# Each half of TensorE's rows makes its own chunks of F, and no PSUM bank has two writers: a change to a routed expert kernel

## Chip, cores and metric

One core of one Trainium2 chip. The metric is the device time of one execution in microseconds (us); the kernel before takes 1424.76 us (median, 1422.38 to 1425.43).

## The reference, cut to what matters

A causal depthwise convolution over 7 positions, then a mixture of 8 experts in which each token goes to one expert.

```python
B, S, D, E, F = (8, 3584, 192, 8, 1024)     # 28,672 tokens
# for each token, with e its expert and p the softmax of its logits:
h = np.maximum(x[b, s] @ w1[e], 0.0)        # first product: 192 -> 1024
out[b, s] = p[e] * (h @ w2[e])              # second product: 1024 -> 192
# e is argmax(logits), or the previous token's expert where the local gate says so
```

Everything is float32. The convolution, the choice of experts and the sorting of tokens into the experts' slots come first for each group of tokens; then blocks of 128 or 256 tokens of one expert run through the two products.

## The kernel before

There are 144 blocks: 35 of 128 tokens, 87 of 256, 22 of 128. TensorE is used as two halves of 64 rows each (`rows = slice(half * 64, half * 64 + 64)`), which run beside each other. `turn` transposes the gathered rows, `hidden` makes the first product and the Relu, `output` the second product in two runs (`part` 0 and 1), `send` scales and scatters. `step` puts pieces of convolution and routing of later groups between the blocks' own work. `P` = 128, `DR` = 64, `FK` = 8 chunks of F, `KT` = 2; `n` is the block's tokens over 128.

```python
    def turn(n, xg):
        xps = xps_p.tile([P, 2, 512], F32, name="xps")
        at = xps.rearrange("p h (d k s) -> p h d k s", d=4, k=2)
        for d in range(2):
            for k in range(n):
                for half in range(2):
                    turn_half(at[:, half, d, k, :],
                              xg[:, k, Y0 + d * P:Y0 + (d + 1) * P], half)
        xT = tp.tile([P, 2, BT], F32, name="xT")
        to = xT.rearrange("p d (k h s) -> p h d k s", k=KT, h=2)
        if n == KT:
            nc.vector.tensor_copy(to.rearrange("p h d k s -> p h (d k) s"),
                                  xps[:, :, :BT].rearrange("p h (x s) -> p h x s", s=DR))
        else:
            nc.vector.tensor_copy(to[:, :, :, 0, :], at[:, :, :2, 0, :])
        return xT
```

192 channels are 128 + 64. To give the last 64 channels a partner on the other half, `xg` holds them twice, and each half takes other chunks of F for them. So in the first product both halves add into the same bank, at different times, and each bank is handed from one half to the other:

```python
    ORDER = [[(0, 0), (1, 0), (0, 1), (1, 1), (4, 0), (5, 0), (2, 0), (3, 0),
              (6, 0), (7, 0), (6, 1), (7, 1)],
             [(2, 0), (3, 0), (2, 1), (3, 1), (6, 0), (7, 0), (0, 0), (1, 0),
              (4, 0), (5, 0), (4, 1), (5, 1)]]
    BANKS = [0, 1, 2, 3]
    def pass_by(last_of):
        seen = nc.scalar.nop()
        for half in range(2):
            tc.add_manual_dep(seen.ins, last_of[half], SYNC, reason="the bank's")
        return seen
    def hidden(n, wb, xT):
        hT = hp.tile([P, FK, BT], F32, name="hT")
        hps = {b: hps_p.tile([P, 2, BT], F32, name="hps") for b in BANKS}
        w = slice(0, n * P)
        left = {b: 6 for b in BANKS}
        passed = {}
        last_of = {}
        for at in range(len(ORDER[0])):
            for half in range(2):
                f, last = ORDER[half][at]
                rows = slice(half * DR, (half + 1) * DR)
                f0 = F + (f % 2 + f // 4 * 2) * P if last else f * P
                b = f // 2
                mm = nc.tensor.matmul(hps[b][:, f % 2, w], lhsT=wb[rows, f0:f0 + P],
                                      rhs=xT[rows, last, w], start=(left[b] == 6),
                                      stop=(left[b] <= 2), skip_group_check=True)
                if at in passed:
                    tc.add_manual_dep(mm.ins, passed[at].ins.name, SYNC, reason="its bank")
                last_of[half] = mm.ins.name
            if at in (3, 5):
                passed[6 if at == 3 else 8] = pass_by(last_of)
            for half in range(2):
                f, last = ORDER[half][at]
                b = f // 2
                left[b] -= 1
                if not left[b]:
                    nc.scalar.activation(hT[:, 2 * b:2 * b + 2, w], hps[b][:, :, w], Act.Relu)
        return hT
    def output(n, wb, hT, yps, part, done):
        for m in range(FK):
            if n == 1 and m // 4 != part:
                continue
            for half in range(2):
                rows = slice(half * DR, (half + 1) * DR)
                k = (part + half) % 2 if n == KT else 0
                mm = nc.tensor.matmul(yps[half if n == 1 else k][:, :D],
                                      lhsT=hT[rows, m, k * P:(k + 1) * P],
                                      rhs=wb[rows, WA + m * D:WA + (m + 1) * D],
                                      start=(m == 0 and not part),
                                      stop=(m == FK - 1 and part == 1), skip_group_check=True)
                if n == KT and part and m == 0:
                    tc.add_manual_dep(mm.ins, done["passed"].ins.name, SYNC, reason="its bank")
                done[half] = mm.ins.name
        if not part and n == KT:
            done["passed"] = pass_by(done)
    def send(n, xg, yps):
        o_sb = op.tile([P, KT, D], F32, name="o_sb")
        for k in range(n):
            gate = xg[:, k, 0:1]
            nc.scalar.activation(o_sb[:, k, :], yps[k][:, :D], Act.Copy, scale=gate)
            if n == 1:
                nc.vector.scalar_tensor_tensor(o_sb[:, 0, :], yps[1][:, :D], gate, o_sb[:, 0, :],
                                               Alu.mult, Alu.add)
            nc.gpsimd.nop()
            # ... indirect DMA of o_sb[:, k, :] to the tokens' rows

```

A hand-over is a ScalarE no-operation that waits for the last matmul of both halves (`pass_by`), and a matmul that waits for it. The second product of a block of 256 has one hand-over as well: in part 0 the first half works for tokens 0 to 127 and the second for 128 to 255, in part 1 the other way round. The loop over blocks:

```python
    for i, (_, n, _, _) in enumerate(blocks):
        ensure(i)
        weights(i + AHEAD)
        hT = hidden(n, wbs[i], xT)
        yps = [yps_p.tile([P, 512], F32, name="yps") for half in range(2)]
        done = {}
        output(n, wbs[i], hT, yps, 0, done)
        if i + 1 < len(blocks):
            xT = turn(blocks[i + 1][1], xgs[i + 1])
        step(0.8 * n, 1)
        output(n, wbs.pop(i), hT, yps, 1, done)
        send(n, xgs.pop(i), yps)
        step(3.2 * n, n)
```

Note the place of `turn`: between part 0 and part 1 of the second product.

## Time and profile before

| | before |
|---|---|
| timed | 1424.76 us |
| first profile, span | 1538.3 us |
| second profile of the same kernel, span (taken later, below) | 1421.5 us |
| late block of 256 / of 128 tokens, start to start | 10.90 / 5.64 us |

The prediction was made from the first profile alone, and its lines are shown there. It was an odd execution, as the experiments found. The same kernel's second profile is the one to compare with; from here on "before" in a profile means the second. Its page opens so:

```profile
span 1421.5 us, 40261 instructions
...
PE 1388.2 (98%) x16670; PEld 1278.9 (90%) x16670; DVE 659.0 (46%) x1773; ACT 497.5 (35%) x1168; POOL 503.6 (35%) x524
```

TensorE is busy all the time but for 33 us, some 20 of them before the first block. Next are its table of waits (total us, times, longest us), first for the waits on ScalarE, and its late blocks in the timeline of TensorE (start, length, line, operation, output and inputs, sizes, count):

```profile
PEld yps L680 <- ACT hT L670: 14.5, 88, 0.4
...
PE yps L680 <- ACT hT L670: 0.2, 1, 0.2
```

```profile
1204.01 5.35 PE L657 MATMUL hps<-xT,wb 64*128 64x256 f32 x48
1209.19 2.90 PE L680 MATMUL yps<-wb,hT 64*128 64x192 f32 x32
1211.93 0.41 PE L263 MATMUL xps<-ident,xg 64*128 64x64 f32 x8
1212.21 2.87 PE L680 MATMUL yps<-wb,hT 64*128 64x192 f32 x32
1214.91 5.35 PE L657 MATMUL hps<-xT,wb 64*128 64x256 f32 x48
```

Read the timeline from start to start. Sixteen steps of the second product take 2.74 us in the first run (1209.19 to 1211.93), where 16 x 0.1625 would be 2.60. And the table of waits has 88 weight loads of the second product (PEld yps) that wait for the Relu, about 0.16 us each: one for nearly every block of 256. The other half is a like wait at the start of the second product in blocks of 128, shown with the run e_first.

### The profile page before, as it was taken

The page shows a single profiled execution, that of the slowest core. Times are in us where ns is not written, and L with a number is a line of the kernel's source. Part 1 is how long each engine was busy: PE and PEld are TensorE (multiplying, and loading weights), DVE is VectorE, ACT ScalarE, POOL GpSimd, SP SyncE. Part 2 cuts the span into 40 slices and gives each one's busy share as a digit, 9 for nine tenths or more (in the row PEclk, how much of TensorE's full clock was granted, in tenths as well). Part 3 has the DMA queues.
Part 4 walks back from the last instruction along what each step waited for, and adds up shares of the span by engine and source line. Part 5 has one row for each costly group of instructions (what it writes and reads, how often), then busy time and mean ns, then how long its engine had stood idle before and what let it go on. Part 6 is the DMA issues. An engine that isn't in the chain of part 4 may idle for free.

```text
span 1538.3 us, 40261 instructions
## 1 busy us (share of the span) xinstructions
PE 1416.7 (92%) x16670; PEld 1278.5 (83%) x16670; DVE 657.0 (43%) x1773; ACT 500.3 (33%) x1168; POOL 502.2 (33%) x524
## 2 busy tenths in 40 slices
PE   7589988999998999999999999998999999999998
PEld 4378988988887787888778887887899999999998
DVE  7557766665665555665565655122000000000111
ACT  3224343342433333343343333322222222222232
POOL 1342335343333334434344343433422121212111
PEclk9899999999999999999999999999999999999999
DMA  4488879866474665656566554555555555556893
GB/s 159 164 318 329 311 280 367 301 268 245 178 281 172 228 223 187 239 192 239 208 222 234 173 193 173 188 171 185 207 206 176 197 183 190 187 180 216 310 322 142
DMA packets 66472, 343.93 MB, mean 224 GB/s; under 512 B 12656, under 2 KB 23655, under 8 KB 45810
## 3 DMA queue, kind: packets, MB, share of 16 engines
q1 hardware_dynamic: 44064, 288.66, 53.4%
q0 software_dynamic: 22224, 52.70, 8.9%
q8 instruction: 131, 2.15, 0.6%
q14 instruction: 51, 0.42, 0.1%
q10 hardware_dynamic: 2, 0.00, 0.0%
HBM read 288.51 MB, written 53.49 MB: 222 GB/s over the span
## 4 chain that ended last, share of the span: by engine, by line
PE 58%; issue 28%; POOL 6%; ACT 4%; another core or an unknown queue 2%; DVE 1%; DMA 0%; POOLq 0%; ACTq 0%; DVEq 0%
PE hps L657 26%; PE yps L680 24%; POOL out_dram L701 4%; ACT hT L670 3%; PE hps L263 2%; PE hps L307 2%; PE xps L263 1%; POOL slots L466 1%; PE yps L184 1%; PE hps L184 1%; DMA x_sb<-in_x_dram 0%; DVE y_sb L201 0%; PE hps L406 0%; POOLq L701 0%
## 5 line engine op out<-in xcount | busy, mean ns | idle before, releaser
L680 PE MATMUL yps<-wb,hT 64*128 64x192 f32 x7392 | 683.7, 330 | 61.5 <-ACT hT L670 45.7
L680 PEld LDWEIGHTS yps<-wb,hT 64*128 64x128 f32 x7392 | 597.3, 187 | 105.4 <-ACT hT L670 72.7
L657 PE MATMUL hps<-xT,wb 64*128 64x256 f32 (+1 forms) x6912 | 648.6, 339 | 22.5 <-ACTq L639 19.6
L657 PEld LDWEIGHTS hps<-xT,wb 64*128 64x128 f32 x6912 | 565.9, 189 | 83.2 <-ACTq L639 29.8
L701 POOL DMA_INDIRECT out_dram<-o_sb,xg x231 | 232.5, 1006 | 902.6 <-ACT o_sb L695 630.1
L670 ACT ACTIVATE hT<-hps 128x512 f32<-128x512 f32 (+1 forms) x576 | 267.3, 511 | 462.4 <-PE hps L657 376.4
L201 DVE SCALAR_TENSOR_TENSOR y_sb<-x_sb,c,y_sb 128x336 f32<-128x336 f32 x720 | 403.2, 570 | 22.4 <-ACT y_sb L176 4.2
L623 DVE COPY xT<-xps 128x512 f32<-128x512 f32 x87 | 60.2, 692 | 611.6 <-PE xps L263 611.6
L466 POOL DMA_INDIRECT slots<-y_sb,posi x224 | 230.4, 1029 | 107.7 <-issue 85.2
L695 ACT ACTIVATE o_sb<-yps,xg 128x192 f32<-128x192 f32 x231 | 87.7, 418 | 360.2 <-PE yps L680 360.2
L626 DVE COPY xT<-xps 128x256 f32<-128x256 f32 x57 | 24.2, 424 | 131.9 <-PE xps L263 123.8
L300 ACT COPY yT<-hps 128x512 f32<-128x512 f32 x93 | 50.1, 592 | 60.5 <-PE hps L263 50.7
L176 ACT ACTIVATE y_sb<-x_sb,c 128x336 f32<-128x336 f32 x116 | 64.8, 580 | 15.1 <-PE yps L680 14.7
L263 PEld LDWEIGHTS xps<-ident,xg 64*128 64x128 f32 x924 | 52.6, 139 | 2.6
L263 PE MATMUL xps<-ident,xg 64*128 64x64 f32 x924 | 52.2, 221 | 0.0
L697 DVE SCALAR_TENSOR_TENSOR o_sb<-yps,xg,o_sb 128x192 f32<-128x192 f32 x57 | 23.8, 418 | 58.0 <-ACT o_sb L695 51.2
L307 PE MATMUL hps<-yT,wg 128*32 128x256 f32 (+1 forms) x384 | 25.9, 376 | 7.4 <-issue 7.4
L307 PEld LDWEIGHTS hps<-yT,wg 128*32 128x32 f32 x384 | 12.1, 111 | 16.2 <-issue 10.8
L263 PE MATMUL hps<-ident,y_sb 64*128 64x64 f32 x512 | 21.2, 223 | 2.6 <-DVE y_sb L201 1.5
L263 PEld LDWEIGHTS hps<-ident,y_sb 64*128 64x128 f32 x512 | 19.8, 139 | 4.0 <-issue 2.7
L184 PE MATMUL hps<-x_sb,wb 128*128 128x336 f32 x56 | 18.1, 489 | 3.7 <-DMA x_sb<-in_x_dram 3.7
L272 POOL COPY yr<-y_sb 128x896 f32<-128x896 f32 x15 | 14.4, 961 | 18.0 <-ACT y_sb L187 18.0
(142 smaller groups left out, 370.3 us busy)
## 6 DMA issues: line engine op xcount, KB each, us to landing
wb<-in_w_dram SPq DMA_DIRECT2D x144, 1536.0 KB
x_sb<-in_x_dram SPq DMA_DIRECT2D x16, 1920.0 KB
xg<-slots SPq DMA_DIRECT2D x87, 258.0 KB
xg<-slots SPq DMA_DIRECT2D x57, 129.0 KB
out_dram<-o_sb,xg POOLq DMA_INDIRECT x231
slots<-y_sb,posi POOLq DMA_INDIRECT x224
slots<-pad SPq DMA_DIRECT2D x1, 129.0 KB
slots<-pad,toi POOLq DMA_INDIRECT x8
```

The costliest lines, as they stand in the source:

```text
L176: nc.scalar.activation(cols(h), chans(h, 0), Act.Copy, scale=c[:, h, 0:1])
L201: nc.vector.scalar_tensor_tensor(cols(h), chans(h, k), c[:, h, k:k + 1], cols(h), Alu.mult, Alu.add)
L263: nc.tensor.transpose(to, src[rows, :], identity=ident[rows, rows])
L300: copy(to[:, :, half * DR:(half + 1) * DR], tps[half])
L307: nc.tensor.matmul(lps[32 * j:32 * j + 32, :w], lhsT=wg[:, u, :], rhs=yT[:, u, j, :w], start=(u == 0), stop=(u == 2))
L466: ins = nc.gpsimd.indirect_dma_start(out=slots[:, :], in_=rows, in_offset=None, out_offset=bass.IndirectOffsetOnAxis(ap=to, axis=0)).ins
L623: nc.vector.tensor_copy(to.rearrange("p h d k s -> p h (d k) s"), xps[:, :, :BT].rearrange("p h (x s) -> p h x s", s=DR))
L657: mm = nc.tensor.matmul(hps[b][:, f % 2, w], lhsT=wb[rows, f0:f0 + P], rhs=xT[rows, last, w], start=(left[b] == 6), stop=(left[b] <= 2), s ...
L670: nc.scalar.activation(hT[:, 2 * b:2 * b + 2, w], hps[b][:, :, w], Act.Relu)
L680: mm = nc.tensor.matmul(yps[half if n == 1 else k][:, :D], lhsT=hT[rows, m, k * P:(k + 1) * P], rhs=wb[rows, WA + m * D:WA + (m + 1) * D], ...
L695: nc.scalar.activation(o_sb[:, k, :], yps[k][:, :D], Act.Copy, scale=gate)
L701: sent = nc.gpsimd.indirect_dma_start(out=out, in_=o_sb[:, k, :], in_offset=None, out_offset=bass.IndirectOffsetOnAxis(ap=xg.bitcast(I32)[ ...
```

## The change

Its intent: no bank has two writers, so no hand-over is needed. Each half holds all 192 channels as three thirds of 64, of overlapping pairs: channels 0 to 63 and 64 to 127, 64 to 127 and 128 to 191, 128 to 191 and again 0 to 63, so that each half sees every third once. It makes its own four chunks of F in its own banks; in the second product each half sums its own rows of all chunks in its own bank, and VectorE adds the two sums. The price is three transposes for two. The transposes move to between the two products, and the stepped-in work is split 2.1 and 2.1 in place of 0.8 and 3.2.

```diff
@@ -610,92 +611,64 @@
 
     def turn(n, xg):
 
+
         xps = xps_p.tile([P, 2, 512], F32, name="xps")
-        at = xps.rearrange("p h (d k s) -> p h d k s", d=4, k=2)
-        for d in range(2):
+        at = xps[:, :, :KD * BT // 2].rearrange("p h (d k s) -> p h d k s", d=KD, k=KT)
+        for d in range(KD):
             for k in range(n):
+                src = xg[:, k, Y0 + d * DR:Y0 + (d + 2) * DR]
                 for half in range(2):
-                    turn_half(at[:, half, d, k, :],
-                              xg[:, k, Y0 + d * P:Y0 + (d + 1) * P], half)
-        xT = tp.tile([P, 2, BT], F32, name="xT")
+                    turn_half(at[:, half, d, k, :], src, half)
+        xT = tp.tile([P, KD, BT], F32, name="xT")
         to = xT.rearrange("p d (k h s) -> p h d k s", k=KT, h=2)
         if n == KT:
             nc.vector.tensor_copy(to.rearrange("p h d k s -> p h (d k) s"),
-                                  xps[:, :, :BT].rearrange("p h (x s) -> p h x s", s=DR))
+                                  at.rearrange("p h d k s -> p h (d k) s"))
         else:
-            nc.vector.tensor_copy(to[:, :, :, 0, :], at[:, :, :2, 0, :])
+            nc.vector.tensor_copy(to[:, :, :, 0, :], at[:, :, :, 0, :])
         return xT
 
-
-
-    ORDER = [[(0, 0), (1, 0), (0, 1), (1, 1), (4, 0), (5, 0), (2, 0), (3, 0),
-              (6, 0), (7, 0), (6, 1), (7, 1)],
-             [(2, 0), (3, 0), (2, 1), (3, 1), (6, 0), (7, 0), (0, 0), (1, 0),
-              (4, 0), (5, 0), (4, 1), (5, 1)]]
-    BANKS = [0, 1, 2, 3]
-
-    def pass_by(last_of):
-
-        seen = nc.scalar.nop()
-        for half in range(2):
-            tc.add_manual_dep(seen.ins, last_of[half], SYNC, reason="the bank's")
-        return seen
+    def halves():
+        return [(half, slice(half * DR, (half + 1) * DR)) for half in range(2)]
 
     def hidden(n, wb, xT):
         hT = hp.tile([P, FK, BT], F32, name="hT")
-        hps = {b: hps_p.tile([P, 2, BT], F32, name="hps") for b in BANKS}
         w = slice(0, n * P)
-        left = {b: 6 for b in BANKS}
-        passed = {}
-        last_of = {}
-        for at in range(len(ORDER[0])):
+
+
+        for two in range(2):
+            hps = [hps_p.tile([P, 2, BT], F32, name="hps") for half in range(2)]
+            for d in range(KD):
+                for j in range(2):
+                    f0 = (d * 4 + two * 2 + j) * P
+                    for half, rows in halves():
+                        nc.tensor.matmul(hps[half][:, j, w], lhsT=wb[rows, f0:f0 + P],
+                                         rhs=xT[rows, d, w], start=(d == 0 and j == 0),
+                                         stop=(d == KD - 1), skip_group_check=True)
             for half in range(2):
-                f, last = ORDER[half][at]
-                rows = slice(half * DR, (half + 1) * DR)
-                f0 = F + (f % 2 + f // 4 * 2) * P if last else f * P
-                b = f // 2
-                mm = nc.tensor.matmul(hps[b][:, f % 2, w], lhsT=wb[rows, f0:f0 + P],
-                                      rhs=xT[rows, last, w], start=(left[b] == 6),
-                                      stop=(left[b] <= 2), skip_group_check=True)
-                if at in passed:
-                    tc.add_manual_dep(mm.ins, passed[at].ins.name, SYNC, reason="its bank")
-                last_of[half] = mm.ins.name
-            if at in (3, 5):
-                passed[6 if at == 3 else 8] = pass_by(last_of)
-            for half in range(2):
-                f, last = ORDER[half][at]
-                b = f // 2
-                left[b] -= 1
-                if not left[b]:
-                    nc.scalar.activation(hT[:, 2 * b:2 * b + 2, w], hps[b][:, :, w], Act.Relu)
+                m = half * 4 + two * 2
+                nc.scalar.activation(hT[:, m:m + 2, w], hps[half][:, :, w], Act.Relu)
         return hT
 
-    def output(n, wb, hT, yps, part, done):
-        for m in range(FK):
-            if n == 1 and m // 4 != part:
-                continue
-            for half in range(2):
-                rows = slice(half * DR, (half + 1) * DR)
-                k = (part + half) % 2 if n == KT else 0
-                mm = nc.tensor.matmul(yps[half if n == 1 else k][:, :D],
-                                      lhsT=hT[rows, m, k * P:(k + 1) * P],
-                                      rhs=wb[rows, WA + m * D:WA + (m + 1) * D],
-                                      start=(m == 0 and not part),
-                                      stop=(m == FK - 1 and part == 1), skip_group_check=True)
-                if n == KT and part and m == 0:
-                    tc.add_manual_dep(mm.ins, done["passed"].ins.name, SYNC, reason="its bank")
-                done[half] = mm.ins.name
-        if not part and n == KT:
-            done["passed"] = pass_by(done)
-
-    def send(n, xg, yps):
+    def output(n, wb, xg, hT):
+
+        yps = [yps_p.tile([P, 512], F32, name="yps") for half in range(2)]
+        for m4 in ([0, 1, 4, 5], [2, 3, 6, 7]):
+            for k in range(n):
+                for m in m4:
+                    for half, rows in halves():
+                        nc.tensor.matmul(yps[half][:, k * D:(k + 1) * D],
+                                         lhsT=hT[rows, m, k * P:(k + 1) * P],
+                                         rhs=wb[rows, WA + m * D:WA + (m + 1) * D],
+                                         start=(m == 0 and k == 0), stop=(m == FK - 1),
+                                         skip_group_check=True)
         o_sb = op.tile([P, KT, D], F32, name="o_sb")
         for k in range(n):
             gate = xg[:, k, 0:1]
-            nc.scalar.activation(o_sb[:, k, :], yps[k][:, :D], Act.Copy, scale=gate)
-            if n == 1:
-                nc.vector.scalar_tensor_tensor(o_sb[:, 0, :], yps[1][:, :D], gate, o_sb[:, 0, :],
-                                               Alu.mult, Alu.add)
+            y = [yps[half][:, k * D:(k + 1) * D] for half in range(2)]
+            nc.scalar.activation(o_sb[:, k, :], y[0], Act.Copy, scale=gate)
+            nc.vector.scalar_tensor_tensor(o_sb[:, k, :], y[1], gate, o_sb[:, k, :],
+                                           Alu.mult, Alu.add)
```

```diff
@@ -816,24 +789,19 @@
         ensure(i)
         weights(i + AHEAD)
         hT = hidden(n, wbs[i], xT)
-        yps = [yps_p.tile([P, 512], F32, name="yps") for half in range(2)]
-        done = {}
-        output(n, wbs[i], hT, yps, 0, done)
         if i + 1 < len(blocks):
             xT = turn(blocks[i + 1][1], xgs[i + 1])
-        step(0.8 * n, 1)
-        output(n, wbs.pop(i), hT, yps, 1, done)
-        send(n, xgs.pop(i), yps)
-        step(3.2 * n, n)
+        step(2.1 * n, 1)
+        output(n, wbs.pop(i), xgs.pop(i), hT)
+        step(2.1 * n, n)
 
 
 def _w1_layout(np, w1):
 
 
-    rest = w1[:, P:, :].reshape(E, DR, FK, P)
-    rest = np.stack([rest[:, :, [0, 1, 6, 7]], rest[:, :, [2, 3, 4, 5]]], 1)
-    rest = rest.reshape(E, P, F // 2)
-    return np.concatenate([w1[:, :P, :], rest], 2)
+    w = w1.reshape(E, KD, DR, 2, F // 2).transpose(0, 3, 2, 1, 4)
+    w = np.stack([w[:, 0], w[:, 1][:, :, [1, 2, 0]]], 1)
+    return w.reshape(E, P, KD * F // 2)
```

(The remaining edits only set sizes and the copied 64 channels.)

More of the change, by code (lines that the diff above doesn't have):

```diff
@@ L31 @@
 NX = NT + HALO
-DR = D - P
+DR = P // 2
+KD = D // DR
 FK = F // P
@@ L54 @@
 GQ = (NP + 3) // 4
-WA = F + F // 2
+WA = F * KD // 2
 WB = FK * D
@@ L262, in turn_half @@
         rows = slice(half * DR, (half + 1) * DR)
-        nc.tensor.transpose(to, src[rows, :], identity=ident[rows, rows])
+        nc.tensor.transpose(to, src[rows], identity=ident[rows, rows])
     def route(g, alone):
@@ L273, in route @@
         if not (alone and g):
-            copy(y_sb[:, :, Y0 + D:], y_sb[:, :, Y0 + P:Y0 + D])
+            copy(y_sb[:, :, Y0 + D:], y_sb[:, :, Y0:Y0 + DR])
         def leave(*pairs):
@@ L312, in route @@
         if alone and g:
-            copy(y_sb[:, :, Y0 + D:], y_sb[:, :, Y0 + P:Y0 + D])
+            copy(y_sb[:, :, Y0 + D:], y_sb[:, :, Y0:Y0 + DR])
         yield "hop"
```

## The prediction

> **What bounds the kernel now.** I read the page first, then the table of waits, then the table of stretches, then the timeline of one late block, in that order.
>
> ```profile
> span 1538.3 us, 40261 instructions
> PE 1416.7 (92%) x16670; PEld 1278.5 (83%) x16670; DVE 657.0 (43%) x1773; ACT 500.3 (33%) x1168; POOL 502.2 (33%) x524
> ...
> DVE  7557766665665555665565655122000000000111
> ```
>
> TensorE is the bound: 92% busy, everything else under half. VectorE works only in the first two thirds, where the convolution and the routing run beside the expert blocks. The first thing to see is the span: the profiled execution took 1538 us, the timed ones 1424.76. The profile is 8% slower than what is to be predicted, so part of what it shows is not in the timed run.
>
> ```profile
> PEld yps L680 <- ACT hT L670: 72.7, 108, 2.3
> ...
> PE yps L680 <- ACT hT L670: 45.7, 57, 2.0
> ...
> PEld hps L657 <- ACTq L639: 29.8, 29, 2.1
> ...
> PE hps L657 <- ACTq L639: 19.6, 21, 1.8
> ```
>
> These are the waits that the change aims at (total, times, longest). The second product (L680) waits for the Relu; the first product (L657) waits for the ScalarE no-operation (L639) that passes a PSUM bank from one half of the rows to the other.
>
> ```profile
> 79.90:327.90 248.00, 226.55 (x3265) 212.09 (x3265) 168.20 (x441) 96.25 (x258) 96.64 (x95) 0.98 0.87 320
> 327.90:1123.00 795.10, 730.73 (x8160) 648.32 (x8159) 402.70 (x1106) 267.71 (x589) 310.59 (x306) 1.00 0.59 206
> 1123.00:1406.90 283.90, 283.90 (x3124) 265.10 (x3122) 17.71 (x26) 75.44 (x156) 51.56 (x53) 1.00 0.54 187
> ```
>
> The columns are stretch, length, busy time of PE, its weight loads, DVE, ACT and POOL, clock, DMA share, GB/s. The first is 35 blocks of 128 tokens, the next two are the 87 blocks of 256 tokens, and 22 blocks of 128 follow. In the third stretch PE is busy for all of its 283.90 us: there are no idle gaps at all. The waits lie in the first two stretches.
>
> ```profile
> 1287.00 5.35 PE L657 MATMUL hps<-xT,wb 64*128 64x256 f32 x48
> ...
> 1292.18 2.91 PE L680 MATMUL yps<-wb,hT 64*128 64x192 f32 x32
> ...
> 1294.92 0.41 PE L263 MATMUL xps<-ident,xg 64*128 64x64 f32 x8
> ...
> 1295.20 2.87 PE L680 MATMUL yps<-wb,hT 64*128 64x192 f32 x32
> ...
> 1297.90 5.35 PE L657 MATMUL hps<-xT,wb 64*128 64x256 f32 x48
> ```
>
> One late block of 256 tokens runs from 1287.00 to 1297.90: 10.90 us. The two row halves run in pairs, so 48 instructions are 24 steps. From start to start: first product 5.18 us (24 steps of 0.216), second product 2.74 (16 steps of 0.1625 are 2.60, and 0.14 over), transposes 0.28 (4 steps of 0.0615, and 0.03 over), second product 2.70 (2.60 and 0.10 over). The single records put the 0.14 at the ninth step of the second product, where it meets the last Relu, and the 0.10 at its first step after the transposes. The same reading of a late block of 128 tokens gives 5.64 us: 24 steps of 0.112, 16 of 0.1625, 2 of 0.0615, and 0.23 over.
>
> **What the Trainium skill says.** "TensorEngine Tiling (Array Packing)", Gotcha 1, PSUM pressure: different row tiles must not be in the same PSUM bank at once, and software has to see to it. That is why the kernel before has its L639 hand-overs, and why a kernel whose halves never share a bank may drop them. "Perfetto Trace Analysis", section on the per-instruction lifecycle: the end of a TensorE instruction in a profile is a model, made from its size. The trace agrees: 48 instructions that start 0.216 us apart in pairs are recorded as 0.376 us each, which is why I count from start to start. "TensorE: Matmul & The Clock Gate", back-to-back issue gap, lists 262 cycles for 256 columns, an estimate of 0.109 us at its 2.4 GHz; the trace has 0.216 for one of the two float32 instructions of a matmul, and I use the trace.
>
> **The change, part by part.**
> 1. Products: the same number and sizes. First product before 12 matmuls per half, after 3 channel thirds by 4 chunks, also 12. Second product 8 chunks per half and 128 tokens in both. Cost 0.
> 2. Transposes: three overlapping pairs of 64 channels instead of two. A block of 256 has 6 steps for 4, a block of 128 has 3 for 2. 87 x 2 x 0.0615 + 57 x 0.0615 = 10.7 + 3.5 = +14.2 us, all on TensorE's path.
> 3. Overheads in a block. The transposes move to between the two products, so the Relu of the first two banks lies behind 2.6 us of first product, and the Relu of the last two behind the transposes and 2.6 us of second product; before, the last Relu had 1.3 us. What stays is the 0.03 at the last transpose and 0.10 after it. Per 256 tokens: 5.18 + 0.37 + 0.03 + 5.20 + 0.10 = 10.88 against 10.90. Per 128: 2.69 + 0.18 + 0.03 + 2.60 + 0.10 = 5.60 against 5.64. Over all blocks: 87 x 0.02 + 57 x 0.04 = about 4 us less, with the 14.2 us of part 2 already paid.
> 4. Stalls. In the single TensorE records I summed each start-to-start distance over its normal step by more than 0.11 us, by place in the block: 60.9 us before the second half of the first run of L680 (Relu of the last banks), 14.6 before its start, 24.9 at the two hand-overs in L657, 7.5 elsewhere; 107.9 in all. The change should take away nearly all of it in the profile, so the profiled span should fall to about 1538 - 100 + a few = 1440 or so. But the timed run hardly has them: 1538.3 - 107.9 = 1430.4, which is already above the timed 1424.76. If every one of these stalls were absent when timed, the sum would still be 6 us too long. In the timelines of the middle stretch ScalarE's semaphore waits are satisfied up to 1.5 us after the matmul they wait for has ended, and in the third stretch 0.05 us after; I read that as delay that profiling adds where many short instructions are recorded. So of the 108 us I allow 5 us (0 to 15) in the timed run.
> 5. Other engines. ScalarE loses 375 hand-overs (2 per block, and 1 per block of 256). VectorE gains 174 additions of the second half at 0.418 us (73 us in all) and the wider xT copy, estimated from 424 ns for 256 and 692 ns for 512 columns as about 0.56 and 0.96 us, together 31 us. A busy block of 256 then gives VectorE 0.96 + 0.84 + 2 x 4.2 (the stepped-in work) = 10.2 us of TensorE's 10.9: under it. Beside, not on the path.
> 6. The end: the last block has 128 tokens and already had both the ScalarE and the VectorE step. No change; start-up likewise.
>
> Sum: 1424.8 - 4 - 5 = about 1415 us.
>
> **Rivals.** (a) The profile is to be believed, and the timed run has the stalls too: then up to 100 us come off and the time is near 1330 to 1380. For it speaks only the table of waits; against it the ledger of part 4, since start-up, blocks without stalls, routing and end already fill the timed span. A weaker form, in which start-up is some 10 us shorter when timed and so 15 to 25 us of stalls remain, gives 1395 to 1402. (b) VectorE becomes the bound in the middle stretch: its additions wait for ScalarE, and the convolution, the routing and the xT copy queue behind them. For it: 10.2 of 10.9 us in busy blocks, 5.2 of 5.6 in blocks of 128. Against: about half of the blocks of a group have little stepped-in work (403 us busy in 795), and the copy of xT has some 4 us to spare because the transposes come earlier. If it bit, +5 to +20 us: 1420 to 1440. (c) The transposes are not paid back: new waits break the run of weight loads after the transposes and at the new Relu waits, 0.1 us each; then the 14 us remain and the time is about 1430. Against: in the trace a wait that is already satisfied costs nothing (the hand-overs of the third stretch). (d) The first stretch is held by DMA (share 0.87 at 320 GB/s): this caps what stalls there could give back, and adds nothing.
>
> **Range and chances.** The centre is 1415. Rival (a), weak, gives the lower end and (b) or (c) the upper: 1400 to 1428 for 8 in 10. Faster by over 2% means under 1396, which needs more stalls in the timed run than the ledger has room for: 0.08. Slower by over 2% is over 1453, where (b) and (c) would have to add up and go wrong beyond their sizes: 0.03. Within 2%: 0.89.
>
> **What would show each step right or wrong.** In the profile after: the profiled span falls several times as much as the timed one (to about 1440); xps transposes count 1386 for 924; the hand-overs and the waits of yps and hps on ScalarE are nearly gone; late blocks start 10.88 and 5.60 us apart; the first step of the second product after the transposes still has its 0.1 us. VectorE's busy time rises by about 100 us without its appearing before TensorE in the waits. I am wrong if the timed run falls by 30 us or more (the stalls were real when timed), or if late blocks take 11.0 us or more (part 3), or if TensorE now waits for xT or for the additions (rival b).

## The result

| | before | after |
|---|---|---|
| timed, median | 1424.76 us | 1413.68 us (1412.24 to 1414.58) |
| ratio | | 0.9924 (0.9907 to 0.9941) |
| profiled span | 1538.3, again 1421.5 | 1412.9 |
| VectorE busy | 659.0 (second profile) | 754.4 |
| late block of 256 / 128 | 10.90 / 5.64 | 10.81 / 5.52 |

A ratio is the mean time of one kernel's runs over that of the other's of the same rounds, so not quite the ratio of the medians quoted. The change is 11 us, 0.8%, faster.

The page of the kernel after opens so:

```profile
span 1412.9 us, 41146 instructions
...
PE 1377.8 (98%) x17132; PEld 1292.3 (91%) x17132; DVE 754.4 (53%) x1947; ACT 488.0 (35%) x1168; POOL 495.5 (35%) x524
```

462 more TensorE instructions (the transposes), 174 more on VectorE, and no other change of the picture. The late blocks of the kernel after, in the timeline of TensorE (same columns as above; L645 is the first product, L264 the transposes, L660 the second product):

```profile
1209.90 5.36 PE L645 MATMUL hps<-xT,wb 64*128 64x256 f32 x48
1215.08 0.55 PE L264 MATMUL xps<-ident,xg 64*128 64x64 f32 x12
1215.45 5.43 PE L660 MATMUL yps<-wb,hT 64*128 64x192 f32 x64
1220.71 1.47 PE L645 MATMUL hps<-xT,wb 64*128 64x256 f32 x12
```

Twelve transposes instead of eight take 0.37 us from start to start. The second product is one run of 5.26 us, where the ideal is 32 x 0.1625 = 5.20; before, its two runs took 2.74 + 2.70 = 5.44. Nothing in the table of waits of the kernel after has the second product (yps L660) waiting for the Relu (hT). The two tables of stretches, for the 35 first blocks and the 87 blocks of 256 (columns: stretch, length, busy time of PE, its weight loads, DVE, ACT, POOL, clock, DMA share, GB/s), before and then after:

```profile
69.90:297.50 227.60, 221.01 (x3265) 210.59 (x3265) 169.52 (x441) 95.50 (x258) 96.25 (x95) 0.98 0.94 363
297.50:1291.20 993.70, 993.70 (x11280) 916.11 (x11279) 420.28 (x1132) 341.44 (x745) 363.16 (x359) 1.00 0.62 218
```

```profile
71.80:292.20 220.40, 213.45 (x3297) 207.64 (x3299) 169.49 (x432) 91.39 (x253) 93.27 (x93) 0.98 0.95 369
292.20:1285.40 993.20, 992.67 (x11673) 931.62 (x11671) 512.56 (x1313) 336.10 (x751) 358.47 (x360) 1.00 0.62 220
```

In the long stretch TensorE is busy all the time in both, and the length is the same, although each late block got 0.09 us shorter: 87 x 0.09 would be 8 us. TensorE has more instructions there (11673 against 11280): 348 are the extra transposes of 87 blocks, and some 40 are routing operations that ran in the first stretch before. So the two stretches are best taken together: 1221.3 us before, 1213.6 after.

To see where the time goes inside the blocks I summed, over the single records of TensorE, by how much each start-to-start distance exceeds its normal step, by place in the block. This is not a view of the profile but arithmetic on the same records; sums in us:

| place | before | after | e_order | e_second |
|---|---|---|---|---|
| 256: ninth step of the second product (meets the last Relu) | 2.5 | 0 | 0 | 0 |
| 256: the step after that | 8.5 | 0 | 0 | 0 |
| 256: last transpose, and the first step of the second product after it | 10.6 | 5.7 | 10.6 | 5.9 |
| 128: start of the second product, its first step (and the last transpose, where it stands there) | 9.6 | 2.8 | 9.3 | 3.4 |
| 128: last transpose and first step after it, where these stand in the middle | 3.9 | 0 | 3.8 | 0 |
| sum | 35.1 | 8.5 | 23.7 | 9.3 |
| transposes over those of before, estimated as 231 x 0.0615 | 0 | 14.2 | 0 | 0 |
| against before | 0 | -12.4 | -11.4 | -25.8 |
| timed, against before (medians) | 0 | -11.1 | -12.7 | -22.4 |

The last two columns are experiments. The table says that the change wins 27 us and gives 14 back.

### The profile page after: what moved, and what is told of

Same layout as the page of the kernel before. It is cut to its first block, busy times and chain, and to the rows that moved or that the text cites. A ratio compares the mean times of both kernels' runs of the same rounds, so it can differ in the third digit from the quotient of the medians. Undisturbed runs are those within 1.5% of the kernel's fastest.

```text
span 1412.9 us, 41146 instructions
## 1 busy us (share of the span) xinstructions
PE 1377.8 (98%) x17132; PEld 1292.3 (91%) x17132; DVE 754.4 (53%) x1947; ACT 488.0 (35%) x1168; POOL 495.5 (35%) x524
## 4 chain that ended last, share of the span: by engine, by line
PE 62%; issue 27%; POOL 6%; DMA 3%; ACT 1%; DVE 1%; POOLq 0%; SPq 0%; ACTq 0%
PE yps L660 26%; PE hps L645 26%; POOL out_dram L674 5%; PE xps L264 2%; PE hps L264 2%; PE hps L308 2%; POOL slots L467 1%; DMA wb<-in_w_dram 1%; PE yps L185 1%; PE hps L185 1%; DMA xg<-slots 1%; DMA x_sb<-in_x_dram 1%; DMA out_dram<-o_sb,xg 0%; DVE y_sb L202 0%; PE hps L407 0%
## 5 line engine op out<-in xcount | busy, mean ns | idle before, releaser
L645 PE MATMUL hps<-xT,wb 64*128 64x256 f32 (+1 forms) x6912 | 635.1, 337 | 1.7 <-DMA wb<-in_w_dram 1.0
L660 PE MATMUL yps<-wb,hT 64*128 64x192 f32 x7392 | 635.8, 325 | 0.0
L645 PEld LDWEIGHTS hps<-xT,wb 64*128 64x128 f32 x6912 | 568.8, 188 | 45.3 <-DVE o_sb L670 5.4
L660 PEld LDWEIGHTS yps<-wb,hT 64*128 64x128 f32 x7392 | 601.1, 188 | 1.1 <-issue 0.9
L202 DVE SCALAR_TENSOR_TENSOR y_sb<-x_sb,c,y_sb 128x336 f32<-128x336 f32 x720 | 412.6, 583 | 22.3 <-ACT y_sb L177 6.6
L650 ACT ACTIVATE hT<-hps 128x512 f32<-128x512 f32 (+1 forms) x576 | 263.9, 510 | 379.9 <-PE hps L645 379.9
L467 POOL DMA_INDIRECT slots<-y_sb,posi x224 | 219.6, 980 | 115.4 <-issue 107.5
L670 DVE SCALAR_TENSOR_TENSOR o_sb<-yps,xg,o_sb 128x192 f32<-128x192 f32 x231 | 88.3, 414 | 293.5 <-ACT o_sb L669 278.2
L625 DVE COPY xT<-xps 128x768 f32<-128x768 f32 x87 | 83.3, 957 | 236.1 <-PE xps L264 236.1
L264 PEld LDWEIGHTS xps<-ident,xg 64*128 64x128 f32 x1386 | 66.4, 140 | 13.6 <-issue 4.5
L264 PE MATMUL xps<-ident,xg 64*128 64x64 f32 x1386 | 67.8, 222 | 5.6 <-DMA xg<-slots 5.6
L628 DVE COPY xT<-xps 128x384 f32<-128x384 f32 x57 | 31.6, 555 | 70.4 <-PE xps L264 70.3
L264 PE MATMUL hps<-ident,y_sb 64*128 64x64 f32 x512 | 21.1, 223 | 2.8 <-DVE y_sb L202 1.7
L264 PEld LDWEIGHTS hps<-ident,y_sb 64*128 64x128 f32 x512 | 19.8, 139 | 4.2 <-ACT y_sb L177 1.8
L185 PEld LDWEIGHTS hps<-x_sb,wb 128*128 128x128 f32 x56 | 12.0, 217 | 10.5 <-issue 6.1
```

The source lines that it names most:

```text
L202: nc.vector.scalar_tensor_tensor(cols(h), chans(h, k), c[:, h, k:k + 1], cols(h), Alu.mult, Alu.add)
L264: nc.tensor.transpose(to, src[rows], identity=ident[rows, rows])
L467: ins = nc.gpsimd.indirect_dma_start(out=slots[:, :], in_=rows, in_offset=None, out_offset=bass.IndirectOffsetOnAxis(ap=to, axis=0)).ins
L645: nc.tensor.matmul(hps[half][:, j, w], lhsT=wb[rows, f0:f0 + P], rhs=xT[rows, d, w], start=(d == 0 and j == 0), stop=(d == KD - 1), skip_g ...
L650: nc.scalar.activation(hT[:, m:m + 2, w], hps[half][:, :, w], Act.Relu)
L660: nc.tensor.matmul(yps[half][:, k * D:(k + 1) * D], lhsT=hT[rows, m, k * P:(k + 1) * P], rhs=wb[rows, WA + m * D:WA + (m + 1) * D], start= ...
```

## The experiments

Eleven runs were made, one of them of the kernel before again; all gave correct results. The theory after the prediction: what the change gains is cover for the Relu, and the extra transposes are a cost with nothing to show for it. The main rival is the intent of the change: what pays is that no bank has two writers.

### The kernel before once more

No edit; the question is whether the 8% between profile and timed run belong to profiling.

> The kernel before, unchanged, for a second profile. The timed run: 1424 us (1422 to 1427), ratio 1.000 within 0.002. Theory P (profiling slows this program whenever it is profiled, because its ScalarE waits stand on the path): the profiled span is again 1525 to 1550 us and the Relu of the last banks again starts 0.9 us late in the middle stretch. Rival (the first profile was one odd execution): the profiled span is 1418 to 1430 us, late blocks as before 10.90 and 5.64 us, and the stalls over 0.11 us sum to under 15 us in place of 108.

Measured: 1423.58 us, ratio 0.9998 (0.9982 to 1.0013), profiled span 1421.5 us. By the single records, the Relu of the last banks in the middle stretch began 0.03 us after its last matmul's recorded end (median), against 0.94 us in the first profile. The execution of the first profile took 1540.02 us as timed, while all other timed executions of this kernel lie between 1421.8 and 1425.7. Theory P falls: this execution was profiled too and was not slowed. The first profile was one odd execution, and why it was odd is not known; its granted clock was 0.989 and that of the second profile 0.990, so the clock is not the reason. Its 108 us of stalls are not the kernel's.

### The second product alone

```diff
 # on the kernel before: hidden() with its shared banks and hand-overs stays, turn() with 2 pairs stays
-    def output(n, wb, hT, yps, part, done):          # two runs, hand-over between
+    def output(n, wb, xg, hT):                       # as after, own bank for each half
+        for m4 in ([0, 1, 2, 3], [6, 7, 4, 5]):
 # loop: turn, step(2.1 * n), output, step(2.1 * n), as after
```

> The first product as before (two whole-bank hand-overs, two overlapping pairs of 64 channels, 4 and 2 transpose steps), the second product and the place of the transposes as after. Theory (the gain is the second product's freedom from a hand-over, which gives the Relu 2.6 us of cover; the 14.2 us of transposes are a pure cost): late blocks 10.68 and 5.46 us, time 1400 us (1396 to 1404). Rival (the hand-overs in the first product cost time in the two stretches with convolution, where ScalarE's queue is full): 1405 to 1415, with stalls at the hand-overs of L657 in the trace.

Measured: 1401.57 us (1399.12 to 1403.48), ratio 0.9839 (0.9826 to 0.9853), late blocks 10.68 and 5.46. Late blocks of 256 in the timeline (L660 is its first product, L683 its second):

```profile
1209.70 5.35 PE L660 MATMUL hps<-xT,wb 64*128 64x256 f32 x48
1214.88 0.41 PE L263 MATMUL xps<-ident,xg 64*128 64x64 f32 x8
1215.13 5.43 PE L683 MATMUL yps<-wb,hT 64*128 64x192 f32 x64
1220.38 1.90 PE L660 MATMUL hps<-xT,wb 64*128 64x256 f32 x16
```

The theory's number and its late blocks came in. The two hand-overs in the first product show no stall of TensorE: it runs its 24 steps in 5.18 us, as the kernel after does without them. This version beats both kernels.

### The first product alone

```diff
 # on the kernel after: hidden() and turn() stay; output(), pass_by(), send() and the loop of before return
-        for m in range(FK):
+        for at, m in enumerate([0, 1, 4, 5, 2, 3, 6, 7]):   # the order in which the Relu's chunks come
```

> The first product as after (own banks, six transposes), the second product with shared banks, its hand-over and the transposes in its middle as before. Theory (the first product's hand-overs cost next to nothing when timed): the transposes add 14.2 us and some of the ninth-step stall goes: 1430 to 1438 us, late blocks near 10.95 and 5.65. Rival (separating the first product's banks is what pays): 1415 to 1425.

Measured: 1412.99 us, ratio 0.9924 (0.9909 to 0.9939), late blocks 10.80 and 5.52. A miss: it is as fast as the whole change. Taken alone it would speak for the rival, separate banks in the first product. But this edit changed two things at once: the banks, and the order in which the second product takes its chunks. The trace has no excess left at the ninth step and after it. The next run shows what the order alone is worth. What the banks did is in the records. A late block of 128 in the second profile of before (L657 is its first product, L670 the Relu of the first two banks, L680 the second product), then in e_first (L645, L650, L667):

```profile
1313.77 2.85 PE L657 MATMUL hps<-xT,wb 64*128 64x128 f32 x48
...
1315.81 0.66 ACT L670 ACTIVATE hT<-hps 128x256 f32<-128x256 f32 x2 [1.43 <-PE hps L657]
...
1316.53 1.57 PE L680 MATMUL yps<-wb,hT 64*128 64x192 f32 x16
```

```profile
1316.50 2.84 PE L645 MATMUL hps<-xT,wb 64*128 64x128 f32 x48
...
1318.09 0.66 ACT L650 ACTIVATE hT<-hps 128x256 f32<-128x256 f32 x2 [0.98 <-PE hps L645]
...
1319.17 1.46 PE L667 MATMUL yps<-wb,hT 64*128 64x192 f32 x16
```

Before, the two Relus end 2.70 us after the start of the block and the second product begins at 2.76; in e_first they end at 2.25 and it begins at 2.67. By the code, the first two banks are complete after 8 of a half's 12 matmuls where they are shared, and after 6 where each half has its own. The later of the two Relus is done 0.42 us ahead there, so the order of chunks plays no part at this place. So own banks in the first product do give something where the second product follows at once: summed as in the table above, the excess at the start of the second product in blocks of 128 is about 10 us before and 0.4 here. The six transposes also give something back in blocks of 256: in those without routing in the middle, the last transpose and the step after it take 0.055 us over their normal steps, against 0.14 with four transposes, so the longer transposes cover more of the hand-over.

### One order alone

```diff
 # on the kernel before, in output()
-        for m in range(FK):
-            if n == 1 and m // 4 != part:
+        for at, m in enumerate([0, 1, 2, 3, 6, 7, 4, 5]):
+            if n == 1 and at // 4 != part:
...
-                                      stop=(m == FK - 1 and part == 1), skip_group_check=True)
+                                      stop=(at == FK - 1 and part == 1), skip_group_check=True)
```

> The kernel before with one edit: the second product takes its chunks in the order 0 1 2 3 6 7 4 5 in place of 0 to 7, so that its ninth step waits for the Relu of the last banks that is issued first, not second. Banks stay shared, hand-overs and 4 transposes stay. Theory R (what the change gains is the wait for the Relu at the ninth step and the slow step after it, 2.5 + 8.5 us of excess in the second profile of before): 1413 us (1411 to 1416), late blocks of 256 at 10.78 in place of 10.90, blocks of 128 still 5.63. Rival B (what it gains is the freedom from banks with two writers): unchanged, 1421 to 1426.

Measured: 1412.22 us (1410.22 to 1412.56), ratio 0.9912 (0.9899 to 0.9926). Its table of waits:

```profile
PEld yps L680 <- ACT hT L670: 0.4, 1, 0.4
PE yps L680 <- ACT hT L670: 0.2, 1, 0.2
```

and a late block of 256:

```profile
1202.84 5.35 PE L657 MATMUL hps<-xT,wb 64*128 64x256 f32 x48
1208.02 2.77 PE L680 MATMUL yps<-wb,hT 64*128 64x192 f32 x32
1210.62 0.41 PE L263 MATMUL xps<-ident,xg 64*128 64x64 f32 x8
```

The 88 waits of 14.5 us became one of 0.4, and the first run of the second product takes 2.60 us in place of 2.74. All banks are still shared and all hand-overs still there. In the kernel before, the Relu of bank 3 (chunks 6, 7) is issued before that of bank 2 (chunks 4, 5), but the second product takes 4, 5 first. It waited for the later of the two by 0.03 us (2.5 us over 87 blocks), and the step after that took 0.098 us longer (8.5 over 87). So a Relu that came a thirtieth of a microsecond late cost four times that, 0.126 us. Taking the last chunks in the order in which the Relu delivers them is worth as much as the whole change, and all of it in blocks of 256: late ones take 10.77 us, those of 128 still 5.64. Rival B falls as an explanation of this gain.

One thing was overlooked. The first two banks stand in the wrong order too: in `hidden` the Relu of bank 1 (chunks 2, 3) is issued before that of bank 0, and the second product begins with chunks 0, 1. In blocks of 256 the Relu has time enough; in late blocks of 128 it ends 2.70 us after the start of the block and the second product begins 0.05 us later, with a first step 0.10 us over its normal length, as at the ninth step of blocks of 256. An order 2 3 0 1 6 7 4 5 on the kernel before was not run; the 9.3 us of excess that stand there in e_order are an estimate of the most that it could give.

### The third pair of transposes alone

```diff
 # on e_second, in turn(): a third pair, made and never read
-        for d in range(2):
+        for d in range(3):
+            d0 = Y0 + (d * P if d < 2 else DR)
```

> The run e_second with the third pair of transposes that the kernel after needs, made and never read: 6 and 3 transpose steps for 4 and 2. Theory (transposes are paid in full on TensorE, 0.0615 us a step, and the first product's own banks give nothing back): e_second plus 14.2 us, 1413 to 1418 us, equal to the kernel after within 2 us. Rival (the first product's hand-overs cost several us, which the kernel after saves): 2 to 6 us above the kernel after, 1417 to 1420; or transposes partly hidden: under 1410.

Measured: 1413.63 us (1412.25 to 1414.94), ratio 0.9921 (0.9907 to 0.9934): 12.1 us above e_second, and the same as the kernel after (1413.68). So the transposes are paid nearly in full, and the first product's own banks, for which they are made, give nothing back here that the runs can see: e_xt has the shared banks, the kernel after does not. This holds where the transposes stand in front of the second product and cover the Relu already; in e_first, where they do not, the first product's own banks did pay. In the profiles of the two, the 87 blocks of 256 take 982.2 us in e_second and 993.1 here; the first 35 blocks 1.7 us more and the last blocks 1.1, which is 13.7 in all.

### The place of the transposes, with the hand-over of the second product

```diff
 # on the kernel before, in the loop
+        if i + 1 < len(blocks):
+            xT = turn(blocks[i + 1][1], xgs[i + 1])
         output(n, wbs[i], hT, yps, 0, done)
-        if i + 1 < len(blocks):
-            xT = turn(blocks[i + 1][1], xgs[i + 1])
         step(0.8 * n, 1)
```

> The kernel before with one edit: the transposes stand between the two products and no longer between the two runs of the second product; the stepped-in work stays where it was. Theory H (the transposes covered the hand-over of the second product's banks; uncovered it costs about 0.3 us in a block of 256, against about 0.2 us won at the Relu, and blocks of 128, which have no such hand-over, win 0.16): 1424 to 1434 us, with a stall of 0.2 to 0.35 us in front of the second run of blocks of 256. Rival (the hand-over costs nothing, the place of the transposes is what counts): 1400 to 1412 us and no such stall.

Measured: 1421.49 us (1419.07 to 1422.72), ratio 0.9971 (0.9956 to 0.9986): below the range by 2.5 us, and far from the rival's. Its table of waits, and a late block of 256:

```profile
PEld yps L680 <- ACTq L639: 16.2, 45, 0.4
```

```profile
1205.97 5.35 PE L657 MATMUL hps<-xT,wb 64*128 64x256 f32 x48
1211.15 0.41 PE L263 MATMUL xps<-ident,xg 64*128 64x64 f32 x8
1211.40 5.80 PE L680 MATMUL yps<-wb,hT 64*128 64x192 f32 x64
1217.04 5.34 PE L657 MATMUL hps<-xT,wb 64*128 64x256 f32 x47
```

The second product takes 5.64 us here, against 5.25 in e_second. The wait for the hand-over (L639) is now on TensorE's path: in 34 blocks the first step of the second run came 0.28 us late (9.5 us in all) and took 0.10 us longer (3.5); in the other 53 a piece of routing stood there and covered it. Blocks of 128 have no such hand-over and fell to 5.46 us. The two nearly cancel, and the range was probably missed because I counted the hand-over for all 87 blocks. So in blocks of 256 the hand-over holds the transposes in the middle as cover.

It would be wrong to call the 1412.22 - 1401.57 = 10.7 us between e_order and e_second (medians of different rounds) the price of that hand-over. From the single records, one profile of each run, in us (the last column runs to the end):

| | first 35 blocks of 128 | 87 blocks of 256 | last 22 blocks of 128 |
|---|---|---|---|
| before (second profile) | 227.6 | 993.7 | 130.3 |
| e_order | 226.0 | 981.7 | 130.3 |
| e_turn | 226.1 | 996.7 | 126.7 |
| e_second | 220.0 | 982.2 | 126.6 |
| e_first | 221.5 | 989.8 | 127.6 |
| after | 220.4 | 993.2 | 127.5 |

Only blocks of 256 have the hand-over, and over all 87 of them e_order and e_second take the same, although the undisturbed late ones differ by 0.09 us (10.77 and 10.68). The difference lies in the blocks of 128, whose second product no longer waits at its start: since transposes stand in front of it (e_turn and e_second), or since the first banks are complete sooner (e_first). In the first 35 blocks the split of the stepped-in work matters as well (230.0 in e_split08, below).

### The place of the transposes, without hand-overs

```diff
 # e_place: on the kernel after, turn() and step(2.1 * n, 1) between the two lists of output()
 # e_place2: the same with the steps 0.8 and 3.2 in place of 2.1 and 2.1
```

> The kernel after with the transposes and the first stepped-in work put back between the two lists of the second product; no bank shared. Theory (cover for the Relu and no hand-over pay, the place of the transposes does not, since the four chunks of the second list still have 2.6 us of cover): 1412 to 1416 us. Rival (moving the transposes to between the products is what pays): 1418 to 1425 us, with the second product starting late after the first.

> The run e_place again with the stepped-in work split 0.8 and 3.2 as in the kernel before, in place of 2.1 and 2.1. Theory (the 7 us that e_place lost came from the routing's small TensorE operations, which met VectorE work stepped in only half a second product earlier): 1412 to 1416 us, and the 12.9 us of excess in front of the routing's operations after the second product fall to 2 or 3. Rival (the place of the transposes itself costs them): 1419 to 1422 us.

Measured: e_place 1420.41 us (1420.10 to 1420.72), ratio 0.9975; e_place2 1412.70 us (1412.36 to 1414.71), ratio 0.9914. Late blocks are 10.80 and 5.52 in both, as in the kernel after: with the chunks in a good order these runs show no difference by the place of the transposes. What cost e_place 7 us is in its table of waits:

```profile
PEld hps L362 <- PE yps L662: 8.1, 10, 0.9
...
PE hps L362 <- DVE keep L356: 5.4, 9, 0.7
...
PE hps L407 <- DVE mine L403: 3.5, 10, 0.4
```

These are the routing's small matmuls. The second and third lines wait for VectorE; the first is of weight loads in front of the same L362 matmuls, whose wait the view puts down to TensorE's own work before. With both pieces of stepped-in work around the second half of the second product, TensorE met the second piece 2.6 us after the first, before VectorE had done it. In e_place2 the first and the third of these lines are gone and the second is a single wait of 2.6 us. My expectation for e_place missed, since I had moved the steps along with the transposes.

### The split of the stepped-in work

```diff
 # on e_second, in the loop: the two numbers of step()
-        step(2.1 * n, 1)  ...  step(2.1 * n, n)
+        step(0.8 * n, 1)  ...  step(3.2 * n, n)     # e_split08
+        step(3.2 * n, 1)  ...  step(0.8 * n, n)     # e_split32
 # e_mixed: 2.1 and 2.1 in blocks of 128, 0.8 and 3.2 (times two) in blocks of 256
```

> The run e_second with the stepped-in convolution and routing split 0.8 before the second product and 3.2 after it, as in the kernel before, in place of 2.1 and 2.1. Theory (e_second still loses about 3 us more than before where routing operations meet TensorE, 14.1 us of excess against 10.8; with the old split fewer routing operations break the run of weight loads): 1397 to 1401 us, late blocks still 10.68 and 5.46. Rival (the split does not matter when no hand-over has to be covered): 1400 to 1403 us.

> The run e_second with the stepped-in work split 3.2 before the second product and 0.8 after it. Theory (as for e_split08: what counts is how many routing operations stand apart, and how long VectorE has had before TensorE meets them): 1397 to 1402 us. Rival (VectorE's long first piece delays the additions of the second half and the copy of xT): 1403 to 1410 us, with TensorE waiting for xT or for the additions.

> The run e_second with the split 2.1 and 2.1 kept in blocks of 128 and the split 0.8 and 3.2 (times two) in blocks of 256. In e_split08 the 87 blocks of 256 took 978.7 us in place of e_second's 982.2, and the first 35 blocks 230.0 in place of 220.0. Theory (the two stretches want different splits and are independent): 1398 us (1396 to 1401). Rival (the loss of e_split08 comes in wherever the first 256 blocks still route, or the gain was noise): 1401 to 1405 us.

Measured: 1407.80 us (0.9887), 1402.76 us (0.9850) and 1404.31 us (0.9867; 1400.27 to 1406.26). None beats e_second. In e_split08 the blocks of 256 did get faster by 3.5 us (978.7 against 982.2), but the first 35 blocks slower by 10 (230.0 against 220.0). e_mixed should have joined the better halves, and timed slower than e_second. Its profiled execution took 1398.6 us, one of its timed ones 1406.3: that single profile would have told another story. The split is left at 2.1 and 2.1.

## Why the prediction was right, and where not

The time was predicted at 1415 and is 1413.7. By its own steps:

1. **Products, no change**: right.
2. **Transposes, +14.2 us**: right within 2 us. Their number is 1386 as predicted, and e_xt measures 12.1 us for them.
3. **Overheads in a block, 4 us less**: right in kind, wrong in size, and this is the term that was mis-sized. I put 10.88 and 5.60 us; they are 10.81 and 5.52. I carried the whole 0.13 us at the transposes over to the new place. Between the products it is about 0.06 us: the excess at the last transpose and after it fell from 10.6 to 5.7 us over 87 blocks. In blocks of 128 I did not see that 0.18 of the 0.23 us over stood at the start of the second product, as a wait for the Relu; after the change about 0.06 are left there. So the term is 87 x 0.09 + 57 x 0.12 = about 15 us with the transposes paid, not 4. What was right is the mechanism in blocks of 256: e_order shows the ninth step's wait for the last Relu, and the slow step after it, as cause.
4. **Stalls**: the conclusion held, its reason did not. The ledger (profile less its stalls is already longer than the timed run) rightly said that the timed run does not have them. That profiling causes them was wrong: the second profile, 1421.5 us, has 11 us of stalls over 0.11 us, and the kernel after 10. So the allowance of 5 us should have been about 1, and the forecast of about 1440 us for the profiled span after was 27 us too long. A term too small by some 11 us and one too large by 4 partly cancelled; with these terms the sum would be -16, and about 5 us of that did not come. The sum had nothing for the places where routing and arriving rows meet TensorE, and these show losses of that size: by the single records, 3.2 us more excess where routing operations stand next to the products of blocks of 256, and a wait for gathered rows of 5.6 us in place of 1.9, since they are transposed earlier. That the number came within 2 us of the measured one is luck in part.
5. **Other engines**: right. VectorE's busy time rose by 95 us (predicted about 100), and TensorE's waits for it stay small: the largest such line in the table of waits of the kernel after is

```profile
PEld hps L645 <- DVE o_sb L670: 5.4, 11, 1.3
```

a weight load ahead of its matmul. Before, the largest such line was 7.2 us.

6. **End and start**: as said, without effect that the runs show.

The rivals: (a), that the profile's waits are in the timed run, is refuted by the second profile. (b), VectorE as bound, did not come. (c), transposes not paid back, was the right worry with the wrong outcome: they are paid back, but mostly by gains that can be had without them, as e_second shows. (d) is not shown: the first stretch fell from 227.6 to 220.4 us while its DMA share stayed at 0.94 to 0.95.

What the prediction did not see is the larger thing. It took the two parts of the change as one price and one gain. The runs show that the gain is time for the Relu, and that it can be had in more than one way: in blocks of 256 by the order of the chunks (12 us), in blocks of 128 by transposes in front of the second product or by own banks in the first. The whole change buys the second of these twice, and pays 12 us of transposes for the own banks. Left open: why the first profile was an odd execution, whether a right order of all four banks would do as much as e_second without any other edit, and what own banks in the first product give beside e_second's arrangement, below the 1 to 2 us that these runs resolve.

## What to carry to other kernels

When the bound engine is busy all the time, look at start-to-start distances at the joints: a consumer that takes its inputs in another order than the producer delivers them costs little per block but in every block, and the cure may be one line. Check every such joint: here the cure was tried at one of two. Take a change apart into what it pays and what pays for it before you keep it: here the second half alone is worth 22 us, twice the whole. And compare the runs stretch by stretch, not by their totals alone: two edits that win as much can win it in different blocks. Last, compare a profile's span with the timed runs before reading its waits; if they differ by several per cent, take another.

## What the Trainium skill lacked or had wrong

- "TensorEngine Tiling (Array Packing)", Gotcha 1: it says that software must keep row tiles out of each other's banks, which these kernels are written to do (no run here tries it without), but gives no price. Here a hand-over by a ScalarE no-operation cost TensorE nothing where other work covered it (the first product takes 5.18 us with and without), and 0.28 us, with 0.10 more in the slow step after it, where none did (34 blocks of e_turn).
- "TensorE: Matmul & The Clock Gate", back-to-back issue gap: the table lists 262 cycles for 256 columns and has no row for float32. The runs show two instructions for each float32 matmul and 0.216 us for each pair of row halves at 256 columns, 0.1625 at 192 and 0.112 at 128. The page says that weight loads are pulled ahead of matmuls, and the trace agrees: in late blocks the second product's loads start 0.16 us before their matmuls. The cost of a wait that interrupts this I found on no page. Here a Relu late by 0.03 us was followed by a step 0.098 us longer than the normal 0.1625, and the load of that step started together with its matmul.
- "Perfetto Trace Analysis": nothing there says that a single profiled execution can be odd. Of the before kernel's two profiles one took 1538.3 us and one 1421.5, with the timed runs at 1422 to 1426.
